# A one-core transformer block: a scaling fixed to VectorE, five output buffers, w4 over the q/k/v weights, and a new order of operations

## The chip, the cores and the metric

The kernel runs on one core of one Trainium2 chip. The metric is the device time of one execution in microseconds (us), lower is better. Before the change three runs took 193.17, 193.51 and 193.54 us, a median of 193.51. The execution that was profiled took 193.18 us.

TensorE is called PE below (its weight loads PEld), VectorE is DVE, ScalarE is ACT, GpSimd is POOL and SyncE is SP. All DMAs of this kernel are issued from SP.

## The reference

The input is x with 2048 rows of 448 bf16 numbers. Everything is computed in this order:

```python
h  = x + A(layernorm(x), wqkv, wo)        # A: attention, 16 heads of 28, each row sees 8 rows: itself, -2, -4 ... -14
h2 = h + B(layernorm(h), w1, w2, w3, w4)  # B: mixer and MLP, with y = layernorm(h):
#   g  = gelu(layernorm(y) @ w1);  quarters of g are shifted along the rows by +1, -1, +2, -2
#   x1 = y + shifted(g) @ w2
#   B  = x1 + gelu(layernorm(x1) @ w3) @ w4          # w3 448 x 1792, w4 1792 x 448
```

Softmax is over the 8 visible rows. Nothing is summed over more than 1792 terms.

## The kernel before, in words

The 2048 rows are worked on in four stages t = 0..3 of 512 rows for the attention and the first half of the mixer, and in five units u = 0..4 of 2, 4, 4, 4 and 2 tiles of 128 rows for the rest. The phases of a stage have short names, which the prediction uses with the stage's number behind them (B11 is phase B1 of stage 1):

- N1: statistics and normalisation of x. A1: the transposes of it and the q and k products. V: the v product; its result `vt` goes by DMA into the layout `vw` (four DMAs for each stage).
- A2: products of q with the shifted k on DVE (`qk_r`, three of 4096 and one of 2048 columns), summed by PE with a 0/1 matrix `zc`. S: the softmax, which ends with the multiplication that writes `pb` (the scaling of p that the title speaks of), 16 small PE transposes of it, and two copies out of PSUM into `pt`.
- A3: DVE spreads `pt` into `bd_r` (four per stage), PE multiplies it with `vw`, and four copies put the result into `actT`. O: the product with wo and the residual into `xin`.
- B1: statistics of `xin`, normalisation into `lntm`, and a DMA transpose of it into `actT`, issued from SP. M: the w1 product and seven gelus of it on ACT (four whole tiles and three shifted pieces) into `arena`.
- B2: the w2 product; DVE adds it to the scaled residual (`arena<-xin,rs_y,ps`) and takes statistics. T: the normalisation and a DMA transpose. POOL adds `xin` to `arena` in place. W3: the w3 product, 14 gelus into `h3T`. B3: the w4 product, DVE's last addition into the output buffer `ost`, and the DMA out.

Each operation of this program is recorded once with its reads and writes (`_Sched.group`), in the order of the phases. `arrange` then takes the operations in the order of a table of 891 numbers (`ORDER`): this is the order in which each engine gets its instructions, and the order in which buffers of the pools are handed out. A second table (`OTHER`) names the operations that run on their second engine: a copy out of PSUM may stand on ACT or on DVE, and a normalisation likewise, and the scaling of p on DVE or on POOL. `_emit_plan` puts a semaphore wait wherever an operation reads what another engine wrote, or reuses its buffer. All engines work through their list strictly in order.

A sum over 448 rows of weights is done by two half-height matmuls at once (`duo`), 64 rows in each half of PE's array; its second half waits for the first. ACT needs one table of functions for Exp and Ln and another for gelu; a load of the other table is put in wherever the kind changes (`emit_engine`). All the compute rows of the profile carry line 987 (after the change 1037), as one helper emits them.

SBUF outside of the pools is one tensor `arena`. In it lie w3, the q/k/v weights, w4, then q (later g) and a part for each stage with k (later p and x1). `NO` is the number of output buffers `ost`.

Of the kernel before, what the change touches and what calls it, by code (L numbers as in the profile page):

```python
# [5 lines left out]
ACT = mybir.ActivationFunctionType  # L6
# [9 lines left out]
NBD, NLN, NACT, NSM, NO = 3, 2, 4, 1, 3  # L16
POWER = {'N1': 'aaaa', 'B1': 'aaaa', 'B2': 'apapp'}
RESIDUAL = 'ttvv'
ORDER = """
# [30 lines left out]
"""  # L50
OTHER = """
104 127 196 197 199 402 408 411 519 525 528 582 583
# [79 lines left out]
class _Sched:  # L132
# [59 lines left out]
    def arrange(self, sequence, other=()):  # L192
# [4 lines left out]
        done = set()  # L197
        self.gorder = []
        for n, k in enumerate(sequence):
# [3 lines left out]
            op.deps |= op.sdeps  # L203
            for d in op.deps | op.odeps:
                if d not in done:
                    raise RuntimeError("operation %d (%s) stands before %d (%s)" % (k, op.tag, d.idx, d.tag))
# [68 lines left out]
def bass_sequential_preLN__sliding_local_dilated__mixer_s_mlp__prompt_kernel(  # L275
# [25 lines left out]
    A_W4 = A_W + 4 * (1344 + 128)  # L301
    A_QG = A_W4 + NF * 448
# [6 lines left out]
    with ExitStack() as es:  # L309
# [17 lines left out]
        st6 = sb("st6", [128, 8, 6], F32)  # L327
        mv = sb("mv", [128, 3, NTL, 2], F32)
# [20 lines left out]
        P_h3 = _Pool("h3", lambda k: h3T[:, k, :], NF + 2)  # L349
        P_st = _Pool("st", lambda k: st6[:, k, :], 8)  # L350
# [70 lines left out]
        def load_x(i, n):  # L421
            return dma("x%d" % i, xin[:, i:i + n, :], xv[:, i:i + n, :], 128 * n * D * 2)

        def load_rows(chan, dst, src, lo, n):

            for h in range(2):
                dma("%s%s" % (chan, "ab"[h]), dst[:, 2 * h:2 * h + 2, :], src[192 * h:192 * h + 256, lo:lo + n].rearrange("(c k) n -> k c n", k=128), 256 * n * 2)
# [24 lines left out]
        for eng in ("sp", "pool", "act"):  # L452
            loads = [op for op in S.ops if op.tag == "load" and op.eng == eng]
            for a, b in zip(loads, loads[1:]):
                b.odeps.add(a)
# [164 lines left out]
        def setup_late(after):  # L620
# [18 lines left out]
            late("memset", ap=vw[0:PADK, 0, 0, :], constant=0.0)  # L639
            late("memset", ap=gT[:, :, 0:2], constant=0.0)  # L640
# [31 lines left out]
        def phase_A1(t):  # L672
# [31 lines left out]
            for h, b in enumerate((X, Y)):  # L704
                copy(qT[64 * h:64 * h + 64, 3, now:now + 256], b(lambda v: v[0:64, 0:256]))
                copy(kr[t][64 * h:64 * h + 64, :, PADK:], b(lambda v: v[64:128, 0:256].rearrange("p (j n) -> p j n", j=4)), False)
            copy(kr[t][64:128, :, 0:PADK], last(X, 0, 4), False)
            copy(kr[t][0:64, 1:4, 0:PADK], last(Y, 0, 3), False)
            if t + 1 < NST:
                copy(kr[t + 1][0:64, 0:1, 0:PADK], last(Y, 3, 1), False)  # L710
# [318 lines left out]
```

## Time and profile before

| | |
|---|---|
| median of three runs | 193.51 us |
| profiled execution | 193.18 us, of which the span of the instructions is 191.7 us |
| PE busy | 181.3 us (95%), 2482 matmuls |
| DVE busy | 129.5 us (68%) |
| ACT busy | 132.9 us (69%), 12 table loads |
| POOL busy | 29.3 us (15%) |
| chain that ended last | 66% PE, 21% ACT, 5% DVE, 2% DMA |

A busy share is over the whole span; the stages differ much, and the prediction reads them one by one. Times in a timeline row are from the span's start; the first number is the start, the second the length, and a bracket at the end of a row gives the idle time ahead of it and what ended it. Neighbouring instructions of an engine overlap a little, so the step from one start to the next is shorter than the length of a row of one instruction.

### The profile page before, as it was taken

What the parts mean: (1) busy time and instruction counts of PE and PEld (TensorE: products, weight loads), DVE (VectorE), ACT (ScalarE), POOL (GpSimd) and SP (SyncE); (2) the same over time, 40 slices, a digit from 0 to 9 for tenths busy, and PEclk for the clock granted to TensorE, in tenths of its full rate; (3) what the DMA queues carried; (4) which work ended last, traced back from release to release, by engine and by line L of the source; (5) the groups of instructions that cost most, each with busy time, mean ns of one, the idle gap of its engine ahead of it and who ended that gap; (6) DMA issues with size and microseconds to landing.
All of it is one profiled execution on the core that took longest, in us unless ns stands there. A gap on an engine that the chain in (4) does not pass through costs nothing.

```text
span 191.7 us, 5740 instructions
## 1 busy us (share of the span) xinstructions
PE 181.3 (95%) x2482; PEld 92.6 (48%) x2482; DVE 129.5 (68%) x229; ACT 132.9 (69%) x310; POOL 29.3 (15%) x63
## 2 busy tenths in 40 slices
PE   6999999999999868989999999999999999999994
PEld 2584533453444333347545444455444544555672
DVE  7799999999999999899876960036988022002203
ACT  4579999999999999999594998860148004821340
POOL 3240000000004000202076000022077600000000
PEclk9999999999999999999999999999999999999999
DMA  5999791004604179480805024006100812000111
GB/s 144 349 268 186 190 320 36 10 3 118 149 3 85 28 64 262 140 178 5 109 3 113 2 50 87 0 3 146 36 27 0 164 51 72 0 3 0 51 48 48
DMA packets 30272, 17.03 MB, mean 89 GB/s; under 512 B 18936, under 2 KB 29736, under 8 KB 30248
## 3 DMA queue, kind: packets, MB, share of 16 engines
q1 hardware_dynamic: 30248, 16.68, 36.7%
q8 instruction: 19, 0.31, 0.7%
q14 instruction: 5, 0.04, 0.1%
HBM read 8.04 MB, written 1.84 MB: 51 GB/s over the span
## 4 chain that ended last, share of the span: by engine, by line
PE 66%; ACT 21%; DVE 5%; DMA 2%; POOL 1%; issue 1%; SPq 1%; POOLq 0%; ACTq 0%
PE ps L987 66%; ACT arena L987 7%; ACT lntm L987 4%; ACT actT L987 2%; DMA vw<-vt 2%; ACT vt L987 2%; ACT L982 1%; DVE lntm L987 1%; DVE st L987 1%; SPq L987 1%; ACT xin L987 1%; ACT ls L987 1%; ACT L987 1%; DVE bd_r L987 1%; DVE actT L987 1%
## 5 line engine op out<-in xcount | busy, mean ns | idle before, releaser
L987 PE MATMUL ps<-actT,arena 64*128 64x256 bf16 (+1 forms) x756 | 68.8, 329 | 1.3 <-DVE arena L987 0.7
L987 ACT ACTIVATE h3T<-ps 128x512 bf16<-128x512 f32 (+1 forms) x70 | 30.3, 525 | 39.3 <-PE ps L987 39.2
L987 PEld LDWEIGHTS ps<-actT,arena 64*128 64x128 bf16 x756 | 35.5, 94 | 30.7 <-PE ps L987 2.1
L987 PE MATMUL ps<-arena,h3T 64*128 64x448 bf16 (+2 forms) x434 | 44.4, 344 | 0.0
L987 ACT ACTIVATE arena<-ps 128x512 bf16<-128x512 f32 (+10 forms) x86 | 40.1, 515 | 3.5 <-PE ps L987 2.8
L987 DVE SCALAR_TENSOR_TENSOR ost<-ps,mrs,arena 128x448 bf16<-128x448 f32 (+1 forms) x17 | 10.6, 652 | 36.4 <-PE ps L987 36.4
L987 DVE TENSOR_TENSOR qk_r<-arena 128x4096 bf16<-128x4096 bf16 (+1 forms) x16 | 32.0, 2017 | 0.7 <-PE ps L987 0.5
L987 PEld LDWEIGHTS ps<-arena,h3T 64*128 64x128 bf16 (+1 forms) x434 | 23.0, 94 | 18.7 <-issue 0.2
L987 POOL TENSOR_TENSOR arena<-arena,xin 128x448 f32<-128x448 f32 x16 | 17.2, 1091 | 45.3 <-DVE lntm L987 45.3
L987 DVE TENSOR_TENSOR bd_r<-arena,bmask 80x2048 bf16<-80x2048 bf16 x16 | 18.9, 1213 | 0.9 <-PE ps L987 0.7
L987 ACT ACTIVATE actT<-ps 128x512 bf16<-128x512 f32 (+2 forms) x21 | 14.6, 743 | 2.1 <-PE ps L987 2.1
L987 PE MATMUL ps<-wo_s,actT 64*128 64x448 bf16 x128 | 14.3, 351 | 0.6 <-DVE actT L987 0.4
L987 PE MATMUL ps<-actT,w_s 64*128 64x512 bf16 x112 | 13.3, 377 | 1.5 <-ACT rs_y L987 0.7
L987 PE MATMUL ps<-arena,actT 64*128 64x448 bf16 x112 | 12.4, 350 | 0.4 <-ACT vt L987 0.4
L987 PE MATMUL ps<-w_s,arena 64*128 64x448 bf16 x112 | 11.6, 350 | 0.9 <-ACT arena L987 0.7
L987 ACT ACTIVATE lntm<-xin,nm 128x448 bf16<-128x448 bf16 x16 | 10.5, 661 | 2.6 <-DVE nm L987 2.6
L987 DVE SCALAR_TENSOR_TENSOR arena<-xin,rs_y,ps 128x448 f32<-128x448 bf16 x16 | 10.3, 672 | 2.1 <-PE ps L987 2.0
L987 DVE TENSOR_SCALAR lntm<-arena,mv,rs_y 128x512 bf16<-128x512 f32 x14 | 10.2, 774 | 2.1 <-POOL rs_y L987 2.0
L987 POOL TENSOR_TENSOR pb<-ls,mx 128x512 bf16<-128x512 f32 x2 | 3.3, 1640 | 52.6 <-ACT mx L987 52.6
L987 DVE BATCH_NORM_STATS2 st<-xin 128x6 f32<-128x448 bf16 x16 | 9.4, 614 | 0.8 <-DMA xin<-in_A_x_dram 0.8
L987 PEld LDWEIGHTS ps<-actT,w_s 64*128 64x128 bf16 x112 | 5.2, 94 | 8.6 <-PE ps L987 1.7
L987 PEld LDWEIGHTS ps<-wo_s,actT 64*128 64x128 bf16 x128 | 5.6, 94 | 7.2 <-PE ps L987 1.4
(73 smaller groups left out, 161.9 us busy)
## 6 DMA issues: line engine op xcount, KB each, us to landing
arena<-in_B_w_dram SPq DMA_DIRECT2D x2, 896.0 KB, 6.7
out_dram<-ost SPq DMA_DIRECT2D x15, 112.0 KB, 1.8
arena<-in_B_w_dram SPq DMA_DIRECT2D x2, 784.0 KB, 5.7
vw<-vt SPq DMA_DIRECT2D x4, 320.0 KB, 4.3
vw<-vt SPq DMA_DIRECT2D x4, 256.0 KB, 4.3
arena<-in_A_wqkv_dram SPq DMA_DIRECT2D x2, 448.0 KB, 5.0
xin<-in_A_x_dram SPq DMA_DIRECT2D x2, 448.0 KB, 7.5
xin<-in_A_x_dram SPq DMA_DIRECT2D x3, 224.0 KB, 5.6
```

Source lines behind the costliest of these rows:

```text
L982: eng.preload_act_table_set("natural_log_exp_and_others")
L987: inst = getattr(eng, meth)(**kw)
```

## The change

Four things differ. The scaling of p is always recorded for DVE; before, stages 2 and 3 had it on POOL. `NO` is 5 instead of 3. w4 no longer has a place of its own in `arena` but lies over the q/k/v weights, so its two loads are recorded behind the v product of stage 3 and follow the last reader of these weights. And the two tables are new. Options for moving the halos, the staged copies and the shifted gelus by DMA (`HALO`, `STAGE`, `COPIED`, `ALONE`) are added and all switched off; an extra tile `stg` of 1 KB per partition is allocated and not used.

The new `OTHER` moves these copies: from ACT to DVE one A1 copy of 128x48 (stage 0), one `actT` copy of 128x16x64 (stage 1), and both `pt` copies of stage 3 (80x512); from DVE to ACT one `actT` copy of A3 of stage 3.

```diff
-NBD, NLN, NACT, NSM, NO = 3, 2, 4, 1, 3
+NBD, NLN, NACT, NSM, NO = 3, 2, 4, 1, 5
+HALO = '....'
+STAGE = '....'
+COPIED = ()
+ALONE = False
 ORDER = """
-43 8 7 2 11 0 1 49 44 45 6 9 10 12 5 39 13 40 42 58 59 60 61 63 64 62 70 68 50 51 52 53 54 55 56 57 14 65 66 71 69 67
+37 5 2 0 3 38 1 4 6 7 39 8 56 57 58 59 47 48 49 50 51 52 53 11 9 61 62 60 63 64 54 55 10 68 66 67 69 70 71 95 65 96 97
...
 OTHER = """
-104 127 196 197 199 402 408 411 519 525 528 582 583
+99 125 132 194 195 197 229 406 409 521 522 528 582 583
...
-    A_W4 = A_W + 4 * (1344 + 128)
-    A_QG = A_W4 + NF * 448
+    A_W4 = A_W
+    A_QG = A_W4 + max(NF * 448, 4 * (1344 + 128))
...
-        w4_v = B_w4.rearrange("(f k) n -> k f n", k=128)
-        for f in range(0, NF, 7):
-            dma("w4%d" % f, w4_s[:, f:f + 7, :], w4_v[:, f:f + 7, :], 128 * 7 * D * 2)
...
-            S.add("dve", "tensor_tensor", alts=[("pool", [("tensor_tensor", mult)])], **mult)
+            dve("tensor_tensor", **mult)
...
+        def load_w4():
+            last = S.ops[-1]
+            w4_v = B_w4.rearrange("(f k) n -> k f n", k=128)
+            for f in range(0, NF, 7):
+                dma("w4%d" % f, w4_s[:, f:f + 7, :], w4_v[:, f:f + 7, :], 128 * 7 * D * 2).odeps.add(last)
...
                     phase(t)
+                    if S.tag == "V%d" % (NST - 1):
+                        S.tag = "w4"
+                        load_w4()
```

What the tables do is seen in the engines' lists at three places. The first is DVE at the softmax of stage 2, from the normalisation of B10 to that of B11. Before:

```order
L987 TENSOR_SCALAR lntm<-xin,nm,rs_y 128x512 x3
L987 TENSOR_REDUCE mx<-ls 128x64
L987 TENSOR_TENSOR qk_r<-arena 128x4096
L987 BN_STATS st<-xin 128x6 x4
L987 BN_AGGR mv<-st 128x2 x4
L987 TENSOR_TENSOR bd_r<-arena,bmask 80x2048 x3
L987 TENSOR_SCALAR lntm<-xin,mv,rs_y 128x512 x4
```

and now:

```order
L1037 TENSOR_SCALAR lntm<-xin,nm,rs_y 128x512 x3
L1037 TENSOR_REDUCE mx<-ls 128x64
L1037 TENSOR_TENSOR qk_r<-arena 128x4096
L1037 TENSOR_TENSOR pb<-ls,mx 128x8x64
L1037 BN_STATS st<-xin 128x6 x2
L1037 BN_AGGR mv<-st 128x2
L1037 BN_STATS st<-xin 128x6 x2
L1037 BN_AGGR mv<-st 128x2 x3
L1037 TENSOR_TENSOR bd_r<-arena,bmask 80x2048 x3
L1037 TENSOR_SCALAR lntm<-xin,mv,rs_y 128x512 x4
```

The multiplication into `pb` is one more instruction of DVE here, ahead of the statistics of B11; the rest keeps its order.

The second is ACT from the first gelus of W30 to those of W31. Before:

```order
L987 ACTIVATE h3T<-ps 128x256 x7
L987 ACTIVATE arena<-ps 80x512 x2
L987 ACTIVATE h3T<-ps 128x256 x7
L987 ACTIVATE actT<-ps 128x512 x2
L982 ACT_TABLE_LOAD
L987 ACTIVATE rs_x<-mv,epsilon 128x4
L987 ACTIVATE rs_y<-rs_x 128x4
L987 ACT_TABLE_LOAD
L987 ACTIVATE arena<-ps 128x512 x2
```

and now:

```order
L1037 ACTIVATE h3T<-ps 128x256 x14
L1037 ACTIVATE arena<-ps 128x512 x2
L1037 ACTIVATE arena<-ps 48x512
L1037 ACTIVATE arena<-ps 128x512 x2
L1037 ACTIVATE actT<-ps 128x512 x3
L1037 ACTIVATE arena<-ps 32x512
L1037 ACTIVATE arena<-ps 16x512
L1032 ACT_TABLE_LOAD
L1037 ACTIVATE rs_x<-mv,epsilon 128x4
L1037 ACTIVATE rs_y<-rs_x 128x4
L1037 ACTIVATE lntm,mv<-xin,nm 128x448 x4
```

The second reciprocal root of B12 (`rs_x`, `rs_y`) moved behind M2's gelus (`arena<-ps`) and shares a table with B13's statistics; the `pt` copies (`arena<-ps 80x512`) are gone from ACT. A second such pair of loads goes the same way at M3, where the root of T2 now stands with one of B13. The list has ten table loads instead of twelve.

The third is SP from B10's transpose to B12's. Before:

```order
L987 DMA vw<-vt 80x4x512
L987 DMA_TRANSPOSE actT<-lntm 128x16x128 x2
L987 DMA vw<-vt 16x3x512
L987 DMA arena<-in_B_w_dram 128x7x448
L987 DMA vw<-vt 16x512
L987 DMA arena<-in_B_w_dram 128x7x448
L987 DMA_TRANSPOSE actT<-lntm 128x8x128
L987 DMA vw<-vt 80x4x512
L987 DMA vw<-vt 64x4x512
L987 DMA_TRANSPOSE actT<-lntm 128x16x128 x3
```

and now:

```order
L1037 DMA_TRANSPOSE actT<-lntm 128x16x128
L1037 DMA vw<-vt 16x512
L1037 DMA vw<-vt 16x3x512
L1037 DMA vw<-vt 80x4x512
L1037 DMA vw<-vt 64x4x512
L1037 DMA vw<-vt 80x4x512
L1037 DMA_TRANSPOSE actT<-lntm 128x16x128
L1037 DMA vw<-vt 16x3x512
L1037 DMA vw<-vt 64x4x512
L1037 DMA arena<-in_B_w_dram 128x7x448
L1037 DMA_TRANSPOSE actT<-lntm 128x8x128
L1037 DMA arena<-in_B_w_dram 128x7x448
```

The transposes are, in this order, those of B10, B11, T0 and B12. Three `vw` moves of stage 2 stood ahead of B10's transpose and now stand behind it, together with two of stage 3; w4's halves (`arena<-in_B_w_dram 128x7x448`) stood ahead of T0's transpose and now stand around it.

More of the change, by code (lines that the diff above doesn't have):

```diff
@@ L197, in arrange @@
         done = set()
+        turned, moved = [], []
         self.gorder = []
@@ L203, in arrange @@
             op.deps |= op.sdeps
+            if not ALONE:
+                pass
+            elif op.insts[0][0] == "dma_start_transpose":
+                op.deps.update(turned + moved)
+                turned, moved = [op], []
+            elif op.is_dma and not callable(op.chan):
+                op.deps.update(turned)
+                moved.append(op)
             for d in op.deps | op.odeps:
@@ L448, in bass_sequential_preLN__sliding_local_dilated__mixer_s_mlp__prompt_kernel @@
         load_rows("w3", w3_s, B_w3, 0, F)
-        w4_v = B_w4.rearrange("(f k) n -> k f n", k=128)
-        for f in range(0, NF, 7):
-            dma("w4%d" % f, w4_s[:, f:f + 7, :], w4_v[:, f:f + 7, :], 128 * 7 * D * 2)
[L452 to L455, printed above, removed]
+        loads = [op for op in S.ops if op.is_dma]
+        for a, b in zip(loads, loads[1:]):
+            b.odeps.add(a)
         TOP, BOT = slice(0, 64), slice(64, 128)
@@ L703, in phase_A1 @@
             duo(half(X, 0, True), half(Y, 64, False), ((0, 256),))
[L704 to L710, printed above, removed]
-                copy(kk[t + 1][:, :, 0:PADK], kk[t][:, :, 512:KVW])
+            if STAGE[t] == "d":
+                stage = _Tile(P_sg)
+                for h, b in enumerate((X, Y)):
+                    copy(stage(lambda v, h=h: v[:, h, :]), b(lambda v: v[:, 0:256]))
+                for h in range(2):
+                    dma("sq%d%d" % (t, h), qT[64 * h:64 * h + 64, 3, now:now + 256], stage(lambda v, h=h: v[0:64, h, :]), 64 * 512)
+                    dma("sk%d%d" % (t, h), kr[t][64 * h:64 * h + 64, :, PADK:], stage(lambda v, h=h: v[64:128, h, :].rearrange("p (j n) -> p j n", j=4)), 64 * 512)
+            else:
+                for h, b in enumerate((X, Y)):
+                    copy(qT[64 * h:64 * h + 64, 3, now:now + 256], b(lambda v: v[0:64, 0:256]))
+                    copy(kr[t][64 * h:64 * h + 64, :, PADK:], b(lambda v: v[64:128, 0:256].rearrange("p (j n) -> p j n", j=4)), False)
@@ new lines, in phase_A1 @@
+            if HALO[t] == "d":
+                if STAGE[t] == "d":
+                    end = lambda h, lo, n: stage(lambda v: v[64:128, h, :].rearrange("p (j n) -> p j n", j=4)[:, lo:lo + n, 64 - PADK:])
+                else:
+                    end = lambda h, lo, n: kr[t][64 * h:64 * h + 64, lo:lo + n, 64:]
+                dma("kra%d" % t, kr[t][64:128, :, 0:PADK], end(0, 0, 4), 64 * 4 * PADK * 2)
+                dma("krb%d" % t, kr[t][0:64, 1:4, 0:PADK], end(1, 0, 3), 64 * 3 * PADK * 2)
+                if t + 1 < NST:
+                    dma("krc%d" % t, kr[t + 1][0:64, 0:1, 0:PADK], end(1, 3, 1), 64 * PADK * 2)
+                    dma("kkc%d" % t, kk[t + 1][:, :, 0:PADK], kk[t][:, :, 512:KVW], 128 * 3 * PADK * 2)
+            else:
+                copy(kr[t][64:128, :, 0:PADK], last(X, 0, 4), False)
+                copy(kr[t][0:64, 1:4, 0:PADK], last(Y, 0, 3), False)
+                if t + 1 < NST:
+                    copy(kr[t + 1][0:64, 0:1, 0:PADK], last(Y, 3, 1), False)
+                    copy(kk[t + 1][:, :, 0:PADK], kk[t][:, :, 512:KVW])
@@ L874, in side @@
                     part = (TOP, BOT)[h]
-                    return [(gT[part, c, 2 + i * 128 + SHIFT[c, h]:130 + i * 128 + SHIFT[c, h]], (lambda lo, m, c=c: w2_s[part, c, lo:lo + m])) for c in range(n)]
+                    return [((gM if h and c in COPIED else gT)[part, c, 2 + i * 128 + SHIFT[c, h]:130 + i * 128 + SHIFT[c, h]], (lambda lo, m, c=c: w2_s[part, c, lo:lo + m])) for c in range(n)]
                 def out():
```

27 lines of the change are left out of this document (20 added, 7 removed), and 58 rows, old and new, of the table ORDER.

## The prediction

> **What bounds the kernel now.** I read the busy shares first, then the engines by stretch of time, then PE's timeline. The page says that PE is busy almost all the time:
>
> ```profile
> PE 181.3 (95%) x2482; PEld 92.6 (48%) x2482; DVE 129.5 (68%) x229; ACT 132.9 (69%) x310; POOL 29.3 (15%) x63
> ```
>
> By stretches (each engine's busy us of 20, then the number of its instructions) three regimes show:
>
> ```profile
> 40.00:60.00 20.00, 19.78 (x444) 9.33 (x444) 19.93 (x22) 19.82 (x57) 0.00 (x1) 1.00 0.27 65
> 60.00:80.00 20.00, 16.63 (x290) 7.03 (x288) 19.30 (x33) 19.39 (x42) 2.20 (x1) 1.00 0.64 138
> 80.00:100.00 20.00, 19.02 (x352) 10.74 (x348) 17.71 (x36) 17.72 (x44) 5.36 (x8) 1.00 0.40 72
> 160.00:180.00 20.00, 20.00 (x226) 10.90 (x224) 1.31 (x3) 8.06 (x18) 0.00 (x0) 1.00 0.09 30
> ```
>
> The columns are PE, PEld, DVE, ACT, POOL, then the granted clock (1.00 throughout). Up to 80 us DVE and ACT both have no rest; from 60 us PE has gaps; late it has none. PE's timeline shows where its last gap is, and what work follows it:
>
> ```profile
> 63.54 3.67 PE L987 MATMUL ps<-actT,w_s 64*128 64x512 bf16 x28 [0.70 <-ACT rs_y L987]
> ...
> 88.46 0.49 PE L987 MATMUL ps<-ident,pb 64*80 64x64 bf16 x16
> 88.92 2.58 PE L987 MATMUL ps<-actT,arena 64*128 64x256 bf16 x42
> 91.34 2.81 PE L987 MATMUL ps<-arena,h3T 64*128 64x448 bf16 x28
> ...
> 98.49 1.50 PE L987 MATMUL ps<-arena,h3T 64*128 64x448 bf16 x14
> 100.41 3.20 PE L987 MATMUL ps<-wo_s,actT 64*128 64x448 bf16 x32 [0.43 <-DVE actT L987]
> 103.45 1.49 PE L987 MATMUL ps<-arena,h3T 64*128 64x448 bf16 x14
> ...
> 107.42 10.74 PE L987 MATMUL ps<-actT,arena 64*128 64x512 bf16 x98
> ```
>
> From 107.42, where W31 begins, PE runs through to its last matmul without a named gap. The change takes no matmul away, and the same ones stand ahead of W31 in both lists: the whole of W30, B30, A33, M2, O3 and B22. So **the time of the new kernel is read from one number, the start of W31**; what it gains or loses on 107.42 is gained or lost at the end.
>
> **The change part by part.** What each engine gets and gives has these rows:
>
> ```profile
> L987 DVE TENSOR_TENSOR pb<-ls,mx 128x512 bf16<-128x512 f32 x2 | 1.4, 683 | 0.0
> L987 POOL TENSOR_TENSOR pb<-ls,mx 128x512 bf16<-128x512 f32 x2 | 3.3, 1640 | 52.6 <-ACT mx L987 52.6
> L987 ACT ACTIVATE actT<-ps 128x1024 bf16<-128x1024 bf16 x6 | 6.2, 1077 | 0.0
> L987 DVE COPY actT<-ps 128x512 bf16<-128x512 bf16 x1 | 0.4, 425 | 0.2 <-PE ps L987 0.2
> L987 ACT ACTIVATE arena<-arena 128x48 bf16<-128x48 bf16 x3 | 0.8, 268 | 0.0
> L982 ACT ACT_TABLE_LOAD x6 | 7.7, 1283 | 0.9 <-PEq L1014 0.8
> ```
>
> *Two table loads less.* 2 x 1.283 = 2.57 us of ACT go. They stood at M2 and M3. PE has no gap at M3, and M2's pair stood behind the last gelus of W30. I take 0 on the path: ACT has idle time there (17.72 of 20). The cover is that idle time and PE's own work of B30 and A33; without it each load would cost its 1.28.
>
> The Trainium skill (ScalarE: Activation LUTs, What ACT_TABLE_LOAD costs) puts a switch at 2.66 us, 1283 ns for the load and the rest for a drain, so two would be worth 5.3. This trace has the same 1283 ns, and no drain behind it is visible here: the load from 86.36 ends at 87.64 and the next activation starts at 87.66 (rows below). Off the path the sum is the same by both; on it the loads would give 2.6 by the rows and 5.3 by the page.
>
> *Early copies onto DVE.* Ahead of B10, DVE gains the copy of 1024 columns and one of 48. The first lies between 0.43 (DVE's own copy of half the width) and 1.08 (ACT's time for it); twice 0.425 less one fixed part, say 0.80. The second lies below 0.27, say 0.15. Sum +0.95. What DVE gives back is its wait here, as the copy that it waited for now stands earlier in ACT's list:
>
> ```profile
> 21.79 5.63 DVE L987 TENSOR_TENSOR qk_r<-arena 128x4096 bf16<-128x4096 bf16 x3 [0.21 <-ACT arena L987]
> ```
>
> So DVE reaches B10 0.74 later. Whether that counts is told by the rows around B10's transpose:
>
> ```profile
> 57.28 1.04 DVE L987 TENSOR_SCALAR lntm<-xin,nm,rs_y 128x512 bf16<-128x512 bf16 x3
> 58.25 0.80 ACT L987 ACTIVATE lntm<-xin,nmr,rs_y 128x512 bf16<-128x512 bf16 x1
> 59.08 2.07 SPq L987 DMA_TRANSPOSE actT<-lntm  x1
> 58.98 2.28 DVE L987 TENSOR_TENSOR qk_r<-arena 128x4096 bf16<-128x4096 bf16 x1
> 60.00 2.20 POOL L987 TENSOR_TENSOR pb<-ls,mx 128x512 bf16<-128x512 f32 x1 [47.91 <-ACT mx L987]
> 64.02 3.49 DVE L987 TENSOR_TENSOR bd_r<-arena,bmask 80x2048 bf16<-80x2048 bf16 x3 [0.21 <-ACT arena L987]
> 66.21 4.30 ACT L987 ACTIVATE arena<-ps 128x512 bf16<-128x512 f32 x8
> ```
>
> Today ACT's normalisation ends last, at 59.05; DVE's ends at 58.32. Now ACT's stands four operations earlier and DVE's would end at 58.32 + 0.74 = 59.06. The transpose leaves at the same time: 0.
>
> *The scaling of p on DVE, stage 2.* DVE pays 0.683 less the 0.07 of overlap seen between neighbours: +0.61. It is queued ahead of the statistics of B11, so their end goes from 63.81 (0.21 before 64.02) to 63.81 + 0.74 + 0.61 = 65.16. ACT waits for them with the root of B11, behind which its gelu table and all of M0's gelus are queued. Three small activations of 0.2 and the table give 65.16 + 0.6 + 1.28 = 67.1, against 66.21 today: M0's gelus are 0.9 later. Nothing is gained for it: POOL's version ended at 62.20, about 1 us behind the end of DVE's `qk_r` from 58.98, and DVE's ends at 62.5.
>
> *On to W30.* DVE carries +0.95 + 0.61 - 0.21 = +1.35 towards T0, and idles 0.7 of the 20 us from 60 to 80, which the delay fills. So +0.65 is left:
>
> ```profile
> 79.69 1.00 DVE L987 TENSOR_SCALAR lntm<-arena,nm,rs_y 128x512 bf16<-128x512 f32 x2
> 82.55 0.65 ACT L987 ACTIVATE lntm<-xin,nm 128x448 bf16<-128x448 bf16 x1
> 86.36 1.28 ACT L987 ACT_TABLE_LOAD   x1
> 87.66 2.04 ACT L987 ACTIVATE h3T<-ps 128x256 bf16<-128x256 f32 x7
> ```
>
> T0's normalisation ends at 81.35. Behind it DVE now has a reduction, a residual, `ls`, a residual and `nm`, 4 x 0.61 + 0.08 = 2.5: 83.87. ACT then takes the four squares of B12 (0.65 each), four small ones (0.7 in all, two of 0.2 and two of 0.15) and the table (1.3): the first gelu of W30 at 83.87 + 2.6 + 0.7 + 1.3 = 88.47, against 87.66. PE has filled the eight PSUM banks by then and waits for two gelus of 0.29: it goes on at 89.05.
>
> *The second scaling of p and the `pt` copies on DVE, stage 3.* Here DVE gains 0.61 + 2 x 0.61 and loses one copy of 0.61. PE does B30's first half and M2 (2.7 + 3.1) ahead of A33 now, which covers it; without that cover A33 would come 1.2 later.
>
> *The rest up to W31.* From 88.92 to 107.42 are 18.50 us. One run of 14 took 1.92 (98.49 to 100.41) where the next took 1.33 (103.45 to 104.78): 0.59 of it was O3's wait for DVE's copy. In the new order PE reaches O3 at 89.05 + 0.35 + 2.4 (W30) + 5.3 (B30) + 3.1 (M2) + 1.4 (A33) = 101.6. DVE reaches the end of that copy from the transposes of S3 (done at about 91.5) over two `pt` copies, four `bd_r` of 1.14, two aggregates, POOL's root (1.1), three normalisations of T1 and the copy itself: 1.2 + 4.6 + 0.3 + 1.1 + 1.4 + 0.6 = 9.2, so at 100.7. It has 0.9 in hand; I leave 0.05 for it. One thing can use that up:
>
> ```profile
> 97.98 1.04 POOL L987 TENSOR_TENSOR arena<-arena,xin 128x448 f32<-128x448 f32 x1
> 97.90 1.86 DVE L987 TENSOR_SCALAR lntm<-arena,mv,rs_y 128x512 bf16<-128x512 f32 x2 [1.14 <-POOL rs_y L987]
> ```
>
> Two normalisations beside POOL's addition took 1.86, where two of the same shape took 1.00 at 79.69. The third of T1's now meets such an addition, ahead of the last `bd_r` and the copy: 0.86 more, just inside the 0.9. The Trainium skill (SBUF — State Buffer, Who interferes with whom) has the two engines share a port pair that one instruction holds for its whole length; by that rule it is the full 1.04 and O3 would be 0.14 late, a sum of 107.5.
>
> The 16 transposes of S3 (0.46 by the steps at 88.46, some of it a wait, say 0.35) now come behind the restart. Sum: 89.05 + 0.35 + 18.50 - 0.59 + 0.05 = 107.36, **0.06 earlier than 107.42**.
>
> *Edits that cost nothing.* Five output buffers: the additions into `ost` wait for PE alone, for 36.4 us in all, so no buffer was short. w4's halves are issued beside T0's transpose, about 81 and 83; the rows:
>
> ```profile
> DVE ost L987 <- PE ps L987: 36.4, 7, 15.3
> arena<-in_B_w_dram SPq DMA_DIRECT2D x2, 784.0 KB, 5.7
> vw<-vt SPq DMA_DIRECT2D x4, 256.0 KB, 4.3
> ```
>
> At 5.7 us to landing the second half is there at 89, B30's second half reads it after 92. The cover is 3 us; without it B30 would wait. Later loads of w1 to w3 have 20 us and more to M0.
>
> The profiled execution took 193.18 for a span of 191.7, so 193.1 is its forecast; the median of the runs shown is 0.33 above it, so the forecast for the median is 193.51 - 0.06, rounded 193.4.
>
> **The rivals.**
>
> *ACT sets the pace, and is relieved (faster).* Between 58 and 74 us the chain of waits names ACT almost alone, and ACT has 1.04 less to do up to W30's first gelu (the two copies of 1.08 and 0.27, less their overlap with neighbours), of which 0.6 is filled up to M0 by small operations drawn ahead. If DVE's extra work fits into its waits, W30's gelus come at 86.6, PE restarts 1.0 earlier, and O3's 0.59 is saved as above, less 0.35 for S3: about -1.3, 192.2. Against it: DVE's 19.93 of 20 between 40 and 60 leave no room. Milder forms end between 192.2 and 193.1.
>
> *DVE's work passes in full (slower).* One mechanism: `pb` stands ahead of B11's statistics, and DVE's +1.35 reaches T0 undiminished, if its 0.7 of idle time between 60 and 80 are waits that the new order keeps. Then W30's first gelu comes at 89.17 and PE restarts at 89.75; and O3's wait stays, as the copies of stage 3 are late as well (0.59). 89.75 + 0.35 + 18.50 = 108.6: +1.2, 194.7. It decides from about 0.5 us of delay beyond mine.
>
> *The late `vw` moves (slower).* Issued behind B10's transpose (from 61.1, 0.6 to 0.7 each), the last one of stage 2 leaves SP at 63.2 and lands at 67.5, if it takes the 4.3 of the row; A32 began at 67.14. Each us more, as the transpose shares the DMA engines, stops PE ahead of M0's second half and so the gelus: at 7 us to landing A32 begins at 70.2, some 1.5 us are lost behind M0, 195.0.
>
> *The change does nothing.* Buffers and w4's place do not show; only the order is left. That is inside my forecast.
>
> **How the numbers follow.** What a measurement of this kernel can tell from no change is about 0.2%, 0.39 us: from 193.12 to 193.90. My forecast has a chance of 0.43; its own error (the copy's 0.43 to 1.08, S3's 0.3 to 0.46, O3's 0 to 0.3) is about 0.4, so 0.37 of it stays within 0.2%, and 0.03 falls on each side. ACT's relief has 0.33, DVE's delay 0.17, the `vw` moves 0.07. Faster 0.36, same 0.37, slower 0.27. The range goes from the faster rival's 192.2 to the slower one's 194.7; the forecast alone has 193.0 to 193.9.
>
> **What would show it.** Right: W31 starts within 0.4 us of 107.42; M0's first gelu near 67.1; the first `h3T` near 88.5; ten table loads; no wait of PE for DVE's `actT` ahead of O3; `pb` on DVE at 0.68. Wrong: a first `h3T` ahead of 87 (ACT was the bound) or behind 89 (DVE passes in full), A32 beginning after 69 with PE waiting for `vw`, or any named gap of PE after W31 begins, where I have none.

## The result and the profile after

The changed kernel takes 194.85 us (median of 20 runs, 194.30 to 197.26) against 193.55 us before (20 runs): a ratio of 1.0079, with a 95% interval of 1.0054 to 1.0104. It is 0.8% slower, where 193.4 was forecast.

In part of the executions of most kernels here the granted clock of TensorE drops to half for some us at about 70 us, so I give, beside the medians of all runs, medians *at full clock*, over the executions with a mean clock of 0.998 or more. They are 194.78 for the change (16 executions of 20) and 193.20 for the kernel before (56 of the 145 that ran beside the experiments): the difference to explain is 1.58 us. The profiled execution of the change has the drop (196.46 us, span 194.7, mean clock 0.982), that of the kernel before has not.

The busy line and the line of the granted clock of the page after:

```profile
PE 182.9 (94%) x2482; PEld 93.2 (48%) x2482; DVE 131.4 (67%) x234; ACT 129.7 (67%) x305; POOL 29.0 (15%) x61
PEclk9999999999999966999999999999999999999999
```

By stretches, with the columns of the table before:

```profile
60.00:80.00 20.00, 17.08 (x264) 6.93 (x264) 17.95 (x30) 17.23 (x38) 2.20 (x1) 0.83 0.72 159
80.00:100.00 20.00, 18.58 (x242) 9.82 (x242) 17.82 (x39) 14.70 (x38) 3.05 (x3) 1.00 0.38 82
140.00:160.00 20.00, 19.33 (x194) 9.22 (x192) 10.38 (x23) 7.28 (x14) 10.55 (x11) 1.00 0.37 62
```

ACT is relieved from 80 to 100 us (14.70 of 20, 17.72 before), and nothing comes of it. Two rows are bad news: the clock of 0.83 from 60 to 80, and PE's 19.33 of 20 from 140 to 160, where it had 20.00 and the prediction has no gap. PE's timeline after:

```profile
63.29 2.79 PE L1037 MATMUL ps<-actT,w_s 64*128 64x512 bf16 x22 [0.60 <-ACT xin L1037]
67.61 0.42 PE L1037 MATMUL ps<-bd_r,vw 80*32 80x64 bf16 x32 [1.54 <-DMA vw<-vt]
67.96 0.82 PE L1037 MATMUL ps<-actT,w_s 64*128 64x512 bf16 x6
71.06 1.68 PE L1037 MATMUL ps<-w_s,arena 64*128 64x448 bf16 x8 [0.54 <-ACT arena L1037]
...
109.42 2.75 PE L1037 MATMUL ps<-actT,arena 64*128 64x512 bf16 x24
...
159.58 11.51 PE L1037 MATMUL ps<-actT,arena 64*128 64x512 bf16 x112 [0.67 <-DMA actT<-lntm]
```

Up to 63 us the two kernels are level (M0 starts at 63.29, before at 63.54). Then come three things: A32 waits 1.54 for the `vw` moves, *ahead* of M0's last six matmuls (67.96); eight matmuls of B20 take 1.68 at half clock; and W33 waits 0.67 at 159.58 for a transpose. The last of these is a named gap behind the start of W31, which the prediction excluded. The chain of waits of the change shows how it comes about:

```profile
145.54 3.26 POOL arena L1037 x3
148.80 0.99 POOL rs_y L1037
...
150.27 3.05 DVE lntm L1037 x3
...
153.34 6.20 DMA actT<-lntm
...
159.58 31.48 PE ps L1037 x343
```

T3's root (`rs_y` of 128x4 on POOL) stands behind three additions of POOL, then come DVE's normalisations, the transposes of T3 and T4 and 6.20 us to their landing. In the kernel before the same steps ran like this (timeline):

```profile
141.79 1.25 POOL L987 TENSOR_TENSOR rs_y<-rs_x,mhalf 128x4 f32<-128x4 f32 x1 [1.36 <-DVE rs_x L987]
...
143.07 4.68 DVE L987 TENSOR_SCALAR lntm<-arena,mv,rs_y 128x512 bf16<-128x512 f32 x5 [0.91 <-POOL rs_y L987]
...
147.78 3.72 SPq L987 DMA_TRANSPOSE actT<-lntm  x2
```

There POOL waited for DVE and took the root at once. The new order draws an addition of T4 and two of T2 ahead on POOL and lets the root queue behind them.

### The profile page after: what moved, and what is told of

It reads as the page before. It is cut to its first block, busy times and chain, and to the rows that moved or that the text cites. A ratio compares the mean times of both kernels' runs of the same rounds, so it can differ in the third digit from the quotient of the medians.

```text
span 194.7 us, 5733 instructions
## 1 busy us (share of the span) xinstructions
PE 182.9 (94%) x2482; PEld 93.2 (48%) x2482; DVE 131.4 (67%) x234; ACT 129.7 (67%) x305; POOL 29.0 (15%) x61
## 4 chain that ended last, share of the span: by engine, by line
PE 59%; DVE 24%; DMA 6%; ACT 4%; POOL 3%; SPq 1%; issue 1%
PE ps L1037 59%; DVE qk_r L1037 8%; DVE bd_r L1037 5%; DMA actT<-lntm 3%; DVE lntm L1037 3%; DVE st L1037 2%; DMA vw<-vt 2%; DVE mx L1037 2%; POOL arena L1037 2%; ACT lntm L1037 1%; DVE ls L1037 1%; ACT arena L1037 1%; DMA xin<-in_A_x_dram 1%; SPq L1037 1%; POOL rs_y L1037 1%
## 5 line engine op out<-in xcount | busy, mean ns | idle before, releaser
L1037 PE MATMUL ps<-actT,arena 64*128 64x512 bf16 (+1 forms) x756 | 69.6, 329 | 2.2 <-ACT h3T L1037 1.1
L1037 POOL TENSOR_TENSOR arena<-arena,xin 128x448 f32<-128x448 f32 x16 | 17.9, 1134 | 44.5 <-DVE lntm L1037 44.5
L1037 PE MATMUL ps<-wo_s,actT 64*128 64x448 bf16 x128 | 15.3, 365 | 0.5 <-DVE ls L1037 0.2
L1037 PE MATMUL ps<-w_s,arena 64*128 64x448 bf16 x112 | 13.6, 377 | 0.7 <-ACT arena L1037 0.5
L1037 POOL TENSOR_TENSOR mrs<-nm,rs_y 128x4 f32<-128x4 f32 x4 | 3.3, 822 | 50.1 <-ACT rs_y L1037 47.8
L1037 PEld LDWEIGHTS ps<-w_s,arena 64*128 64x128 bf16 x112 | 5.4, 98 | 7.2 <-ACT arena L1037 1.8
```

What stands on the lines that cost most here:

```text
L1037: inst = getattr(eng, meth)(**kw)
```

## The experiments

The theory to begin with: the late root costs 0.7 to 0.9 us. The rival: the loss is made by the late `vw` moves, the prediction's slower rival with a chance of 0.07. In the diffs a number is an operation of the order.

### The root ahead of the additions (the change with one entry moved)

```diff
-780 781 847 ... 849 717 716 782 846 784      # 782: T3's root; 849, 717, 716: additions
+780 781 782 847 ... 849 717 716 846 784
```

> The changed kernel with one entry of its order moved: the root of T3 (POOL's rs_y of 128x4) stands directly behind the DVE operation that feeds it, ahead of the three POOL additions behind which the change had put it. Late-root theory (POOL's three additions, 3.26 us, stand ahead of T3's root, so the transposes of T3 and T4 leave 3 us late and PE waits 0.67 ahead of W33): the root ends near 146, the transposes leave near 150 and land near 156, PE reaches W33 without a wait, and the kernel is 0.7 to 0.9 us faster than the change alone: 194.0, ratio to the kernel before about 1.003. Late-vw theory (the loss is made by the vw moves of stage 2 ahead of M0's second half): no change in time, 194.8, ratio 1.008. Either way everything ahead of 140 us is as in the change, so this profile also shows where W31 starts when the granted clock is not lowered: 107.4 to 107.8 if only the root is to blame, 108.5 or more if the vw moves cost their 1.5.

Measured: 194.02 us, ratio 1.0033 (1.0011 to 1.0054); at full clock 194.00, **0.78 less than the change**. Its timeline:

```profile
67.95 0.42 PE L1036 MATMUL ps<-bd_r,vw 80*32 80x64 bf16 x32 [1.65 <-DMA vw<-vt]
69.16 2.58 ACT L1036 ACTIVATE arena<-ps 128x512 bf16<-128x512 f32 x5 [0.65 <-PE ps L1036]
89.32 2.25 PE L1036 MATMUL ps<-actT,arena 64*128 64x256 bf16 x36 [0.45 <-ACT h3T L1036]
107.80 10.10 PE L1036 MATMUL ps<-actT,arena 64*128 64x512 bf16 x92
142.56 1.79 POOL L1036 TENSOR_TENSOR rs_y<-rs_x,mhalf 128x2 f32<-128x2 f32 x2 [12.97 <-DVE mv L1036]
143.31 5.76 DVE L1036 TENSOR_SCALAR lntm<-arena,mv,rs_y 128x512 bf16<-128x512 f32 x6 [0.54 <-POOL rs_y L1036]
149.09 3.72 SPq L1036 DMA_TRANSPOSE actT<-lntm  x2
157.15 11.50 PE L1036 MATMUL ps<-actT,arena 64*128 64x512 bf16 x112
```

Both roots run at 142.56, the transposes leave at 149.09, and W33 begins with no wait. This execution had the full clock, and up to 140 us it is the change itself: W31 starts at 107.80. So of the 2.0 us that W31 is late in the profile of the change (109.42), some 1.6 belong to that execution's clock, not to the change. The wait for `vw` is still there (1.65), and ACT stands still for 0.65 in M0's gelus because of it.

### The vw moves ahead of the transpose, alone and with the root

```diff
-197 198 499 385 384 383 501      # 198: B10's transpose; 385, 384, 383: stage 2's vw moves
+197 385 384 383 198 499 501
```

> The changed kernel with stage 2's three late vw moves issued ahead of B10's transpose instead of behind it. Late-vw theory: A32's wait of 1.54 us for vw is gone, M0's second half and its gelus come 0.6 to 1.5 us earlier, W31 starts 0.6 to 1.5 us earlier and the kernel takes 193.3 to 194.2 (ratio 0.999 to 1.004). Late-root theory: the wait goes, but another (ACT's gelus, DVE's chain) ends at the same place, or the gain is given back at W33, where the transposes of T3 and T4 come late whatever PE did: at most 0.3 us, ratio 1.006 to 1.008.

Measured: 194.47, ratio 1.0055 (1.0032 to 1.0077); at full clock 194.46, 0.32 less than the change. The gap before W33 stays:

```profile
157.01 11.51 PE L1036 MATMUL ps<-actT,arena 64*128 64x512 bf16 x112 [0.58 <-DMA actT<-lntm]
```

So the late root shows as a wait of PE of 0.58 here and 0.67 in the profile of the change; what its repair gives beyond that, up to 0.78, is within the 0.2 that a median is good to.

> Both moves together: T3's root ahead of the additions and stage 2's vw moves ahead of B10's transpose. If the two losses are separate and add up: 0.7 to 0.9 from the root and what the vw moves gave by themselves, so 192.7 to 194.0; if the late root takes up what the vw moves give, this kernel gains more than the sum of the two single ones. Late-root alone: as with the root alone, 194.0, ratio 1.003.

Measured: 193.53, ratio 1.0001 (0.9985 to 1.0016). The same kernel once more beside other runs:

> The changed kernel with both repairs once more, beside the others, so that the scaling of p in stages 2 and 3 is compared on the same chip: 193.5, ratio 0.999 to 1.001; if the run with stage 2's scaling on POOL gained nothing but a better chip, this one shows 0.998 too.

Measured: 193.87, ratio 1.0010 (0.9994 to 1.0026). Both together at full clock: 193.68 over 24 executions on two chips (193.53 and 193.87). From the root alone (194.00) that is 0.32 again, or 0.47 on the one chip that ran both, so **the two losses add up, 0.78 and some 0.3 to 0.5**. The timeline with both repairs (of the first of the two runs):

```profile
66.65 4.31 ACT L1036 ACTIVATE arena<-ps 128x512 bf16<-128x512 f32 x8
66.91 0.42 PE L1036 MATMUL ps<-bd_r,vw 80*32 80x64 bf16 x32 [0.76 <-DVE bd_r L1036]
88.04 2.04 ACT L1036 ACTIVATE h3T<-ps 128x256 bf16<-128x256 f32 x7
88.75 2.25 PE L1036 MATMUL ps<-actT,arena 64*128 64x256 bf16 x36 [0.68 <-ACT h3T L1036]
107.29 10.10 PE L1036 MATMUL ps<-actT,arena 64*128 64x512 bf16 x92
```

The wait of 1.65 for `vw` does not vanish, 0.76 of it becomes a wait for DVE's `bd_r`; ACT's eight gelus of M0 run without a stop. W31 starts at 107.29, 0.5 ahead of the run with the root alone; the prediction has 107.36.

### Why a wait of 1.6 us costs 0.3

```diff
-205 411 206 414      # 411: A32's first 32 matmuls; 205, 206: M0's
+205 206 411 414
```

> The changed kernel with T3's root repaired, the vw moves still late, and A32's first 32 matmuls put behind M0's last six instead of ahead of them. With the root alone the kernel took 194.02, with root and vw 193.53. If the wait for vw costs because it stands ahead of M0's last six and so holds back the last gelus (ACT idles 0.56 there): A32 still waits, 0.9 to 1.3, ACT's idle 0.56 is gone, and the kernel takes 193.5 to 193.6, ratio 1.000. If A32's own lateness counts (its bd_r, actT and O2 behind it): 194.0, ratio 1.003.

Measured: 193.87, ratio 1.0029 (1.0001 to 1.0057); at full clock 193.75, against 194.00 with the root alone (on another chip) and 193.87 with early moves (on the same chip).

```profile
63.24 3.67 PE L1036 MATMUL ps<-actT,w_s 64*128 64x512 bf16 x28 [0.59 <-ACT xin L1036]
67.58 1.14 PE L1036 MATMUL ps<-bd_r,vw 80*32 80x64 bf16 x96 [0.66 <-issue]
66.55 4.31 ACT L1036 ACTIVATE arena<-ps 128x512 bf16<-128x512 f32 x8
```

The moves leave SP as late as in the change and A32 begins at 67.58 (the profile names no releaser for its wait of 0.66), but M0 is done and ACT's gelus run through. At full clock the kernel is level with the one with early moves. The medians do not separate the two readings by themselves; the rows do.

The late moves alone, in the kernel before:

```diff
-200 480 505          # 200: B10's transpose; 387, 385, 386: stage 2's vw moves
+200 387 385 386 480 505
```

> The kernel before with one thing done as in the change: stage 2's three vw moves of 0.6 to 0.7 us each are issued behind B10's transpose (59.08) instead of before 50 us. They land near 67.5. In this order A32 stands behind all 28 matmuls of M0, at 67.14. Theory that the order of PE makes the price (in the change, A32 stands ahead of M0's last six, so that its wait holds back M0's gelus): A32 waits 0.3 to 0.8 here, part of it in the place of the 0.45 that it waits for DVE at its second piece, M0's gelus are not held back, and the kernel takes 193.5 to 193.8, ratio 0.999 to 1.001. Theory that the late vw costs its half microsecond wherever A32 stands: 194.1, ratio 1.0025.

Measured: 193.73, ratio 1.0007 (0.9987 to 1.0027). The three moves leave from 60.68 and land in time:

```profile
60.68 2.46 SPq L986 DMA_DIRECT2D vw<-vt  x3
66.89 0.42 PE L986 MATMUL ps<-bd_r,vw 80*32 80x64 bf16 x32
```

No wait at all: here three moves stand behind the transpose, where the change has five (60.75, 4.05 us of issue), and A32 stands behind M0. Late moves alone cost nothing here; with two more of them and A32 drawn ahead they cost 0.3 to 0.5.

### The late root alone, and later still

```diff
-742 782 847 783      # the kernel before
+742 847 849 717 716 782 783
```

> The kernel before with one thing done as in the change: T3's root on POOL is put behind three additions (two of T2, one of T4). Nothing else is changed. Late-root theory: the root ends about 3.2 us later (near 146 instead of 143), the transposes leave near 151 instead of 147.8 and land near 157.2, PE waits 1.3 to 1.8 us ahead of W33 (155.43 before), and the kernel takes 194.9 to 195.4, ratio 1.007 to 1.009. If the order on POOL does not matter: 193.5, ratio 1.000.

Measured: 193.86, ratio 1.0012 (0.9988 to 1.0035), less than expected; at full clock 193.69 (9 executions), 0.5 above before. The profiled execution has the steps as foreseen:

```profile
142.52 3.01 POOL L986 TENSOR_TENSOR arena<-arena,xin 128x448 f32<-128x448 f32 x3 [1.81 <-DVE lntm L986]
145.49 1.02 POOL L986 TENSOR_TENSOR rs_y<-rs_x,mhalf 128x4 f32<-128x4 f32 x1
150.38 3.74 SPq L986 DMA_TRANSPOSE actT<-lntm  x2
156.55 1.90 PE L986 MATMUL ps<-actT,arena 64*128 64x512 bf16 x16 [0.67 <-DMA actT<-lntm]
```

The transposes leave 2.6 us later, not 3.2, since DVE's five normalisations behind the root take 3.81 and not 4.68, with fewer additions beside them. PE waits the same 0.67 as in the change. The order on POOL alone makes the gap. Put into the kernel before it costs 0.5, taken out of the change it gives 0.8; what makes these two differ is not shown.

```diff
-847 ... 849 717 716 782 846      # the change; 846, 848: T4's second normalisation and its addition
+847 846 ... 849 848 717 716 782
```

> The changed kernel with T3's root put one POOL addition later still: T4's second normalisation and its addition also stand ahead of the root, so four additions stand there instead of three. Late-root theory: the root, the normalisations, the transposes of T3 and T4 and W33 all come one addition (1.0 us) later, nothing else can absorb it, and the kernel is 0.9 to 1.1 us slower than the change: 195.8, ratio to before 1.0115 to 1.014. If the root's place costs only part of what is put down to it (the profile's 0.67 us is taken up elsewhere): under 0.5, ratio below 1.011.

Measured: 196.97, ratio 1.0130 (1.0083 to 1.0177). At full clock only two executions of six remain, 194.82 and 195.30, 0.3 above the change and not 1.0. The timeline shows what took it up (everything here is 0.5 later than in the profile of the change: T4's root ran at 144.67 against 144.16):

```profile
146.04 4.24 POOL L1036 TENSOR_TENSOR arena<-arena,xin 128x448 f32<-128x448 f32 x4 [0.66 <-DVE lntm L1036]
150.25 1.02 POOL L1036 TENSOR_TENSOR rs_y<-rs_x,mhalf 128x4 f32<-128x4 f32 x1
151.30 2.63 DVE L1036 TENSOR_SCALAR lntm<-arena,mv,rs_y 128x512 bf16<-128x512 f32 x4 [4.88 <-POOL rs_y L1036]
153.96 3.84 SPq L1036 DMA_TRANSPOSE actT<-lntm  x2
```

The root runs 1.0 later, as foreseen, but DVE's four normalisations behind it take 2.63 where the change has 3.50: the addition no longer runs beside them. The transposes leave 0.1 later by the same count, and PE waits 0.81 instead of 0.67. By these rows an addition is paid once, ahead of the root or beside the normalisations; "nothing else can absorb it" was wrong.

### The scaling of p

Both repairs, and stage 2's scaling back on POOL (a second form for the operation, and its number, 400, in the list `OTHER` of those that take it):

```diff
-            dve("tensor_tensor", **mult)
+            S.add("dve", "tensor_tensor", alts=[("pool", [("tensor_tensor", mult)])], **mult)
```

> The changed kernel with both repairs (root ahead of the additions, stage 2's vw moves ahead of B10's transpose), and stage 2's scaling of p back on POOL, where the kernel before had it. The repaired kernel takes 193.5. If the 0.61 us on DVE stands on the path to M0 and W30, as the prediction's term has it: PE's wait of 0.76 for bd_r ahead of A32 shrinks by 0.6, M0's gelus come 0.6 earlier, and the kernel takes 192.9 to 193.1 (ratio 0.997). If DVE's work there is hidden behind ACT: 193.5, ratio 1.000. If the addition beside DVE's work slows DVE down: above 193.7.

Measured: 193.23, ratio 0.9977 (0.9960 to 0.9994); at full clock 193.23, against 193.68 with the scaling on DVE. PE's wait ahead of A32 is 0.49 where it was 0.76, and the first `h3T` comes 0.27 earlier:

```profile
66.58 0.42 PE L1036 MATMUL ps<-bd_r,vw 80*32 80x64 bf16 x32 [0.49 <-DVE bd_r L1036]
87.77 2.04 ACT L1036 ACTIVATE h3T<-ps 128x256 bf16<-128x256 f32 x7
```

Stage 3's operation (519) joins that list:

> The changed kernel with both repairs, and the scaling of p of stage 3 back on POOL as well as that of stage 2. With stage 2's alone the kernel took 193.23, ratio 0.9977. If stage 3's 0.61 on DVE is covered, as the prediction has it (B30's first half and M2 stand ahead of A33): the same 193.2, ratio 0.997 to 0.999. If it is not: up to 0.6 faster, 192.6. If POOL's 1.64 us beside DVE's work, or the later p, costs more than it saves: 193.5 and more.

Measured: 193.92, ratio 1.0022 (0.9995 to 1.0049); at full clock 193.26. No difference to stage 2's scaling alone is shown (193.23), as the prediction has it, but the two ran on different chips, between which the kernel with both repairs differs by 0.3. On the same chip as this run that kernel, with both scalings on DVE, took 193.87. **By the medians stage 2's scaling on DVE costs about 0.4**; the rows of its profile show 0.27 of it at the first `h3T` and 0.17 at W31 (107.12 against 107.29).

### The parts of the code without the new order

The change's code with the order of before, w4's loads behind stage 3's last `vw` move:

```diff
-NBD, NLN, NACT, NSM, NO = 3, 2, 4, 1, 3
+NBD, NLN, NACT, NSM, NO = 3, 2, 4, 1, 5
-    A_W4 = A_W + 4 * (1344 + 128)
+    A_W4 = A_W
```

> The kernel before with its own order of operations, and of the change only two parts: five output buffers instead of three, and w4 in the place of the q/k/v weights, so that its two loads are issued behind stage 3's last vw move. The scaling of p stays where it was. The prediction has 0 for both: 193.5, ratio 0.999 to 1.001, no wait of PE for w4. If w4 comes too late for B30: PE waits for it near 92 us and the kernel is slower by that wait. If the buffers were short: faster.

Measured: 195.66, ratio 1.0105 (1.0074 to 1.0135); none of the six executions had the full clock.

```profile
83.91 2.22 SPq L1036 DMA_DIRECT2D arena<-in_B_w_dram  x2
94.42 1.50 PE L1036 MATMUL ps<-arena,h3T 64*128 64x448 bf16 x14 [1.09 <-DMA arena<-in_B_w_dram]
```

Both halves of w4 are issued from 83.91, and B30 waits 1.09 for them. In the new order the first half goes out at 72.96 and the second at 84.83, and nobody waits: w4's new place is free only because the order brings stage 3's moves forward. (Two runs below with w4's new place and three buffers took 195.20 and 194.53 at full clock, four executions each: 1.3 to 2.0 above the kernel before.)

> The kernel before with its own order of operations and all parts of the change but the new order: five output buffers, w4's new place, and the scaling of p on DVE in stages 2 and 3 too. If DVE's 2 x 0.61 us stand on the path to W30: 194.1 to 194.8, ratio 1.003 to 1.006, with the first h3T 0.6 to 1.2 later than 87.66. If they are hidden: 193.5, ratio 1.000. The difference to the run without the scaling is the price of that part.

Measured: 198.01, ratio 1.0215 (1.0172 to 1.0258). PE waits for DVE at two new places:

```profile
63.04 0.61 PE L1036 MATMUL ps<-qk_r,zc 128*32 128x512 bf16 x8 [1.42 <-DVE qk_r L1036]
92.58 0.49 PE L1036 MATMUL ps<-ident,pb 64*80 64x64 bf16 x16 [1.09 <-DVE pb L1036]
```

In the old order stage 2's scaling stands ahead of `qk_r` and waits 0.88 there for ACT itself. Five of the six executions had a lowered clock, so the 2.3 us between these two runs is no clean price; the two waits do show that the scaling on DVE needs another order than the old one.

### What lies around the span

Time minus span is 1.456 us on average before (1.39 to 1.53 in 145 executions) and 1.777 after (1.73 to 1.81 in 20); with the order of before and the change's code it is 1.722. So 0.32 of the 1.58 us are in no row of any profile.

```diff
-NBD, NLN, NACT, NSM, NO = 3, 2, 4, 1, 5      # the run with the change's code and the old order
+NBD, NLN, NACT, NSM, NO = 3, 2, 4, 1, 3
```

> The kernel before with its own order, and of the change only w4's new place (three output buffers, as before, and so 46 semaphores; the run with five buffers had 48). What lies around the span (time minus span) was 1.455 us before, 1.72 with w4's place and five buffers. If it is the two more semaphores of the two more output buffers: back to 1.45. If it is w4's later load: 1.72. The wait of PE for w4 (1.09) stays either way, and the time is 195.4 or 195.7.

Measured: 1.475 around the span; 195.06 in all, ratio 1.0076 (1.0048 to 1.0105), with PE's wait for w4.

```diff
+        spare = [es.enter_context(nc.semaphore("spare%d" % i)) for i in range(3)]
```

> The kernel before with three more semaphores that no instruction uses. If what lies around the span grows with the semaphores that a kernel owns: 1.455 + 3 x 0.135 = 1.86 us. If only semaphores that are used count, or none: 1.455. The span stays at 191.7 to 192.2.

Measured: 1.467 around the span, 193.54, ratio 1.0009 (0.9980 to 1.0038).

```diff
+SHARE = {'x0': 'out0', 'x1': 'out4', 'x2': 'out1', 'x4': 'out2', 'x6': 'out3', 'x8': 'out4b'}
+                op.chan = SHARE.get(op.chan, op.chan)      # for every load
```

> The changed kernel with both repairs and stage 2's scaling on POOL (193.23, 1.775 us around the span, 48 semaphores), in which six early loads count on the semaphores of the six output channels, which are first used 80 us later: 42 semaphores, and nothing else changed. If each used semaphore costs 0.135 us around the span (0.27 for the two that the change added): 1.775 - 6 x 0.135 = 0.97, and 192.4 us, ratio to before 0.9935. If the semaphores cost nothing: 1.775 and 193.2, ratio 0.998.

Measured: 1.781 around the span, 193.40, ratio 1.0012 (0.9986 to 1.0037).

In the next, eight more loads (of `wo` and the q/k/v weights) join `SHARE`:

> As the run before, with eight more early loads on semaphores that other transfers use much later: 34 semaphores. If each costs 0.135 us around the span: 1.775 - 14 x 0.135 would be below zero, so the price must end somewhere: under 0.9 us, 192.3 or less. If the number of semaphores has nothing to do with it: 1.775 and 193.2.

Measured: 1.769 around the span, 193.41, ratio 1.0019 (0.9992 to 1.0046).

```diff
         ost = sb("ost", [128, NO, D], BF16)      # NO = 3
+        spare = sb("spare", [128, 2, D], BF16)
```

> As the run with w4's new place and three output buffers (1.475 us around the span), with room set aside in SBUF for two more buffers that nothing uses. If the room that the buffers take makes the 0.27 us around the span: 1.72 to 1.75. If it is their use (two more channels whose last transfer SP waits for at the end): 1.475. The time stays at 194.5 to 195.5, with PE's wait for w4.

Measured: 1.444 around the span, 195.09, ratio 1.0067 (1.0034 to 1.0101).

```diff
-            if e == "sp":
+            if e in ("sp", "act"):
+                last = [op.chan for op in order["sp"]][-2:]
                 for c, v in out_final.items():
-                    eng.wait_ge(chan_sems[c], v)
+                    if (c in last) == (e == "sp"):
+                        eng.wait_ge(chan_sems[c], v)
```

> The changed kernel with both repairs and stage 2's scaling on POOL (193.23, 1.775 us around the span), in which SP, at the end, waits for the last transfers of two of the six output channels, and ScalarE for the other four, instead of SP for all six. If each wait at SP's end costs 0.135 us: 1.45 or less around the span, and 192.7 to 192.9, ratio to before 0.995 to 0.996. If the ends of the channels cost nothing: 1.775, and 193.2 to 193.4.

Measured: 1.734 around the span, 0.04 less than without this edit, where the kernel before had 1.445 beside it; 193.15, ratio 0.9971 (0.9947 to 0.9995).

It is the *use of five output buffers*: in the order of before, taking two back gives 0.25 back. It is not the number of semaphores and not the room in SBUF, and moving four of the six last waits from SP to ACT gives 0.04. How two more buffers lengthen what no profile shows stays open.

## Why the prediction was wrong, step by step

At full clock, each step from the medians above. One of them is good to about 0.2: the kernel before took 193.13 to 193.50 beside the different experiments.

| step | time | difference |
|---|---|---|
| the change | 194.78 | |
| T3's root ahead of POOL's additions | 194.00 | -0.78 |
| stage 2's vw moves ahead of the transpose | 193.68 | -0.32 |
| stage 2's scaling back on POOL (31 executions of three kernels that differ in semaphores alone) | 193.31 | -0.37 |
| the kernel before | 193.20 | -0.11 (the span 0.25 longer, what lies around it 0.32 shorter) |

- **The step that failed** is the first: "the time of the new kernel is read from one number, the start of W31". PE ran without a gap behind W31 *in the order before*, and the prediction carried that over. The new order also rearranges POOL's list at 145 us, and with it DVE's and SP's, and there a root of 1.0 us came to stand behind 3.26 us of additions whose results nobody awaits soon. PE waited 0.58 to 0.67 ahead of W33 for the transposes behind it, and taking the root ahead gave 0.78 back. No row of before warns of it; the new order, read on POOL up to the end, does. This is the largest part, and the prediction had no rival for it.
- **The late vw rival** was named with a chance of 0.07, and its landing (67.5) was right: A32 began at 67.61. What was mis-sized is its condition: the prediction set the landing against 67.14, A32's start behind all of M0. In the new order PE reaches A32 at 66.07, behind 22 of M0's 28 matmuls, so that a move "in time" stopped PE for 1.54. For this landing the prediction names no price (its 1.5 is for a landing 7 us after the issue); it was 0.3 to 0.5, and not the whole 1.54, since 0.76 of the wait becomes another one.
- **The scaling of p in stage 2** was charged with 0.61 of DVE; it costs about 0.4. The early copies were charged with 0.74, and DVE came only 0.28 later (`qk_r` starts at 59.26 against 58.98), so B11's statistics end near 64.5, not 65.16, and M0's first gelu comes at 66.57, not 67.1. Against stage 3's scaling at no price no run speaks.
- **The path to W31** held in its times: with both mishaps repaired first `h3T` 88.04 (88.47 predicted, over-charged by the early copies), PE on again at 88.75 (89.05), no wait for `actT` ahead of O3, W31 at 107.29 (107.36); as changed, 107.80. That 107.29 is so close to 107.36 is in part luck. PE is on again 0.30 earlier than predicted and takes 0.23 longer from there, and what released W31, after some 0.1 without work on PE, is no term of the sum: T1's fourth normalisation and the transpose behind it, as the chain of waits with both repairs shows.

```profile
100.88 0.80 DVE lntm L1036
...
101.70 5.54 DMA actT<-lntm
...
107.29 80.81 PE ps L1036 x833
```

From 83.79 on this chain is DVE's work, but for short steps between the engines and one root on POOL. The new order has put DVE where ACT stood: in the chain that ended last, ACT had 21% and DVE 5% before, and the page of the change has

```profile
PE 59%; DVE 24%; DMA 6%; ACT 4%; POOL 3%; SPq 1%; issue 1%
```

- So ACT's relief, the faster rival with 0.33, gave nothing: it would have shown in a first `h3T` ahead of 87, which did not come. Ten table loads are left; no run takes the two fewer by themselves, and the chain above does not pass where they stood on ACT.
- **Five buffers at 0** was wrong by about 0.3, outside the span. The prediction took what lies around the span as fixed. **w4's place at 0** was right in this order only.
- The rival "DVE's work passes in full" gave a time near the one measured, 194.7, by another path: its two marks, a restart of PE at 89.75 and O3's wait, did not come.
- The prediction lets the third normalisation of T1 meet an addition of POOL. It met none (0.54). The fourth did (0.87, so 0.33 more, where 0.86 was charged), behind the copy for O3, which it left alone, but on the chain to W31 above. With the Trainium skill (SBUF — State Buffer, Who interferes with whom), by which one engine's instruction holds the shared port pair for its whole length, this agrees in kind: normalisations beside additions took 0.96 each in the run with the repaired root (5.76 for six), and 0.50 alone.

The three repaired kernels with stage 2's scaling on POOL took 193.23, 193.40 and 193.41, against 193.20 for the kernel before at full clock: level with it and faster than the change. The best median of all, 193.15 (0.9971, up to 0.9995), is that of the run with the split waits, 193.14 at full clock. Over all executions this and the 193.23 lie just below the kernel before, which has the lowered clock more often; the two between them do not, so a gain over before is not shown.

## What to carry to other kernels

When an order is searched anew, read the whole new list of each slow, in-order engine against the old one, up to the end of the program: a stretch in which the bound engine had no gap shows slack that belongs to the old order. A transfer that lands "in time" is compared with the moment at which its reader now gets its turn, not with the one in the profile before, and behind a bound engine's early wait one asks whose input is held back. Time minus span is a number of its own, and worth comparing first, since it varies by 0.1 us where the time varies by three.

## What the runs showed of the hardware

In some executions the granted clock falls to 0.50 for one stretch, which begins between 69 and 73 us. In the profile of the change, columns as above:

```profile
70.00:72.00 2.00, 1.46 (x14) 0.53 (x8) 2.00 (x2) 1.95 (x5) 0.00 (x0) 0.50 0.84 162
72.00:74.00 2.00, 2.00 (x42) 0.80 (x40) 0.55 (x1) 1.96 (x4) 0.00 (x0) 0.50 0.91 171
74.00:76.00 2.00, 2.00 (x12) 0.51 (x8) 1.41 (x6) 0.42 (x2) 0.00 (x0) 0.50 0.79 134
```

It comes in two lengths, and the mean clocks of the execution are 1.00, about 0.991 or about 0.982. Here it is about 6.8 us (the clock is 0.82 from 68 to 70 and 0.98 from 76 to 78); in the run of the change's code in the old order, with 0.989, it is about 3.4 us (0.50 from 70 to 72, 0.64 from 72 to 74). The kernel before had it in 89 of 145 executions (median 193.81 against 193.20 without), the change in 4 of 20 (196.46 to 197.26), the change with both repairs in none of 24. What sets it off is open. It begins near the time at which PE is least busy (0.46 of 2 us from 66 to 68 in the change), but the profile of the run with the root alone has 0.35 there and keeps the full clock. And the repaired kernel with both scalings on POOL differs from the one with stage 2's only behind 85 us, and had it in 5 of 12 executions, the other in none, though on another chip.
